# A new written order for the head and the first thirteen tiles of an attention and channel-mix kernel

## The chip, the cores and the metric

The kernel runs on one core of a Trainium2 chip. The metric is the device time in microseconds of one execution. A core has five engines, each with a queue of its own that is worked off in order: PE (matmul), DVE (vector), ACT (scalar, with exponentials), POOL (a second, slower vector engine) and SP (which issues transfers here). Engines wait for each other by semaphores.

## The reference

Attention over keys that are pooled 4 by 4, and a channel mix of its output. There are 4 batches of 12,288 tokens with 128 channels; the keys of a batch, which are also its values, are 768.

```python
kv_pool = kv.reshape(B, H // r, r, W // r, r, C).mean(axis=(2, 4))
k = v = kv_pool.reshape(B, -1, C) @ w_sr
s = scale * (q @ k.transpose(0, 2, 1))
a = np.exp(s - s.max(-1, keepdims=True)); a /= a.sum(-1, keepdims=True) + 1e-09
x = a @ v
x_prev = x shifted by one token
xk = mu_k * x + (1.0 - mu_k) * x_prev
xr = mu_r * x + (1.0 - mu_r) * x_prev
k = np.maximum(xk @ w_k, 0.0)                 # 128 -> 1024
out = 1.0 / (1.0 + np.exp(-(xr @ w_r))) * (k * k @ w_v)
```

## The kernel before, in words

The tokens are worked on in 97 tiles: the first 512 tokens as two tiles of 256 (0 and 1), then 95 tiles of 512. All products are made with operands split in a high and a low part, so most matmuls come in threes (high by low, low by high, high by high).

A tile goes through these steps; the names stand in the tables of the order and, in part, in the trace. *Scores:* load `qf` (SP), split it into `qh` (ACT) and `ql` (POOL); for each 128 tokens s the scores `S0` to `S3` on PE, their maximum `nm` (DVE), the exponential `ex` (ACT, the trace's `pe`), the reciprocal of the sum `rc` (two small DVE instructions), and the normalised weights in two parts, `f1` (ACT) and `f2` (DVE), both `pp` in the trace; `tt` transposes them by DMA into `pT`. *Values:* `AV0` to `AV5` on PE (`px`). *Mix:* `xek` and `xer` on ACT scale `px` by the token scales `s`; `xk` and `xr` on DVE add the shifted part; `xkh`, `xrh` (DVE) and `xkl`, `xrl` (POOL) split them. *Channel mix*, for four groups f of 256 hidden channels: `ha`, `hb` on PE (`ph`), `r` on ACT (`rr`), the product `k2` on DVE (`kk`, or `ph` in place, for one group on ACT), its split `kh` and `kl`, and `va`, `vb` on PE (`pv`). *Gate:* `z` on PE (`pz`), `E` and `th` on ACT, `E1`, `T1` and `g` on DVE, the product `o` on DVE, the store `so`.

Tiles 0 to 8 take their scores from `ksh`, `ksl` and `ksb`. From tile 9 on ACT scales `qf` first (`qs`), POOL clips it (`qg`), and the scores come from `vv`, the scaled keys in two parts. All else is the same.

Ahead of the tiles stands the head: the weights are loaded and split (`wvh`, `wkl` and so on), the first batch's keys and values are loaded, pooled and projected (`pa`, `pb` on PE with fillers of `warm`), split (`ksh`, `ksl`, `ksb`), and the scales are found: `am`, the maximum over the keys (`ex<-ks` in the trace), `ex`, `exi`, `es`, `ivs` after it, `vv` from these; `dg`, `xm` (POOL and PE), `xt` and its reciprocal `xi` (DVE), and `sv` with `s` (POOL) for the token scales. `busy0` and `busy1` are 7 and 6 matmuls of 256 columns (`pw`) whose result nobody reads.

Buffers go round in rings: PSUM has three buffers called `big` (scores, `ph`, the pooled keys), one for `px`, `pz` and `xm`, one for `pv`. In SBUF there are 2 of `qf`, `qh` and `ql`, 4 of `pe` and `pp`, 2 of `pT`, 3 of `kk`, 4 of `kh` and `kl`, 2 of `rr`.

What sets the order is a table of numbers. Each step is put into a heap under its number (lines 68 to 79), and all are issued from the smallest number to the largest; `Ordered` (lines 33 to 45) keeps that order on each engine. The number is a place in the order, not a time at which something happens. `ONCE` (line 921) holds the head's numbers, `EARLY` those of the first tiles, one table for each, `WHEN` those of every later tile, to which i times `PERIOD` is added for tile i, and `LATE` those of the last four. A table also decides which buffer a step gets, since rings hand out theirs in the order of issue.

```python
    def add(self, when, name, fn, of):
        heapq.heappush(self.heap, (when, next(self.count), fn, name, of))
    def give(self):
        while self.heap:
            heapq.heappop(self.heap)[2]()
```

Of the kernel before, what the change touches and what calls it, by code (L numbers as in the profile page):

```python
# [1239 lines left out]
```

## Time and profile before

| | us |
|---|---|
| median of 3 executions | 1860.04 |
| the three | 1862.19, 1859.86, 1860.04 |
| the profiled execution | 1862.46 |
| its span (first to last instruction) | 1860.70 |
| outside the span | 1.76 |
| PE busy | 1844.8 (99%) |
| DVE busy | 1765.7 (95%) |
| ACT busy | 1715.5 (92%) |
| POOL busy | 1229.2 (66%) |

The granted TensorE clock is 0.999 of full over the span. All steps have line 43 in the trace, since one helper records them; instructions are told apart by their tile's name. A row of a timeline has the start, the duration, the engine, the operation with its output and inputs, and in brackets how long the engine had been idle ahead of it and who ended that. Neighbouring instructions of one engine overlap a little in these rows: the start of one to the start of the next is some hundredths of a microsecond less than a duration. In rows of the scores and of `ph` the output is named by its buffer's step.

The span has a head of some 28 us to the first scores, a stretch up to some 210 us in which the first eleven or so tiles come into step, the steady stretch of 18.8 us per tile, and a tail of some 20 us.

### The profile page before, as it was taken

What the parts mean: (1) busy time and instruction counts of PE and PEld (TensorE: products, weight loads), DVE (VectorE), ACT (ScalarE), POOL (GpSimd) and SP (SyncE); (2) the same over time, 40 slices, a digit from 0 to 9 for tenths busy, and PEclk for the clock granted to TensorE, in tenths of its full rate; (3) what the DMA queues carried; (4) which work ended last, traced back from release to release, by engine and by line L of the source; (5) the groups of instructions that cost most, each with busy time, mean ns of one, the idle gap of its engine ahead of it and who ended that gap; (6) DMA issues with size and microseconds to landing.
All of it is one profiled execution on the core that took longest, in us unless ns stands there. A gap on an engine that the chain in (4) does not pass through costs nothing.

```text
span 1860.7 us, 27187 instructions
## 1 busy us (share of the span) xinstructions
PE 1844.8 (99%) x9175; PEld 903.8 (49%) x9175; DVE 1765.7 (95%) x2554; ACT 1715.5 (92%) x2448; POOL 1229.2 (66%) x885
## 2 busy tenths in 40 slices
PE   8999999999999999999999999999999999999999
PEld 5544444444444444444444444444444444444444
DVE  7999999999999999999999999999999999999997
ACT  6999899999999999999999999999999999999997
POOL 2565666676667676767667676767676767676665
PEclk9999999999999999999999999999999999999999
DMA  7866566555556666655656566655574556555552
GB/s 247 157 132 148 117 131 131 108 119 117 119 110 143 135 144 137 129 110 112 124 108 142 131 147 133 145 117 113 105 129 102 119 108 114 113 110 117 103 108 57
DMA packets 644380, 232.16 MB, mean 125 GB/s; under 512 B 612368, under 2 KB 613392, under 8 KB 644240
## 3 DMA queue, kind: packets, MB, share of 16 engines
q1 hardware_dynamic: 644240, 230.43, 59.2%
q8 instruction: 72, 1.18, 0.3%
q14 instruction: 68, 0.56, 0.1%
HBM read 52.63 MB, written 25.17 MB: 42 GB/s over the span
## 4 chain that ended last, share of the span: by engine, by line
PE 85%; DVE 2%; ACT 1%; issue 1%; POOL 0%; DMA 0%; SPq 0%; ACTq 0%; DVEq 0%
PE pv L43 24%; PE ph L43 23%; PE px L43 17%; PE S L43 17%; PE pz L43 3%; DVE pp L43 0%; ACT pp L43 0%; ACT rr L43 0%; DVE nm L43 0%; PE pk L43 0%; ACT pe L43 0%; ACT kh L43 0%; DMA qf<-qT 0%; ACT kk L43 0%; DVE xr L43 0%
## 5 line engine op out<-in xcount | busy, mean ns | idle before, releaser
L43 POOL TENSOR_TENSOR kl<-kk,kh 128x1024 bf16<-128x1024 f32 (+1 forms) x291 | 681.6, 2343 | 51.9 <-DVE kh L43 14.6
L43 DVE SCALAR_TENSOR_TENSOR pp<-pe,rc,pp 128x768 f16<-128x768 f32 x384 | 430.4, 1140 | 3.6 <-ACT pp L43 0.9
L43 PE MATMUL px<-pT,vT 128*128 128x512 f16 (+1 forms) x1746 | 422.0, 378 | 1.1 <-DMA pT<-pp 1.1
L43 ACT ACTIVATE rr<-ph 128x1024 f32<-128x1024 f32 (+1 forms) x388 | 389.1, 1004 | 17.4 <-PE ph L43 16.1
L43 DVE TENSOR_REDUCE nm<-S 128x1 f32<-128x768 f32 x384 | 363.1, 947 | 39.2 <-PE S L43 37.6
L43 ACT ACTIVATE pe<-S,nm 128x768 f32<-128x768 f32 x384 | 344.3, 897 | 43.4 <-DVE nm L43 41.6
L43 ACT ACTIVATE pp<-pe,rc 128x768 f16<-128x768 f32 x384 | 338.8, 927 | 40.4 <-ACT pe L43 37.3
L43 PE MATMUL S<-vv,qg 128*128 128x512 f16 (+1 forms) x1408 | 324.7, 326 | 0.0
L43 ACT ACTIVATE kh<-rr 128x1024 f16<-128x1024 f32 (+1 forms) x291 | 303.6, 1044 | 8.9 <-ACT rr L43 0.4
L43 PE MATMUL pv<-kh,wvl 128*128 128x512 f16 (+1 forms) x784 | 292.6, 375 | 2.4 <-DVE o L43 2.4
L43 PE MATMUL ph<-xkh,wkl 128*128 128x512 f16 (+1 forms) x776 | 292.4, 377 | 1.1 <-ACT pe L43 0.9
L43 PE MATMUL pv<-kh,wvh 128*128 128x512 f16 (+1 forms) x784 | 292.6, 375 | 0.0
L43 PE MATMUL ph<-xkh,wkh 128*128 128x512 f16 (+1 forms) x776 | 292.3, 377 | 0.0
L43 PEld LDWEIGHTS <-vT 128*128 128x128 f16 x1746 | 171.1, 98 | 201.7 <-issue 1.7
L43 POOL TENSOR_SCALAR qg<-qf 128x512 f16<-128x512 f32 x88 | 82.3, 935 | 266.5 <-ACT qf L43 266.5
L43 DVE TENSOR_TENSOR kk<-ph,rr 128x1024 f32<-128x1024 f32 (+1 forms) x194 | 233.8, 1205 | 5.6 <-ACT rr L43 5.3
L43 POOL TENSOR_TENSOR xrl<-xr,xrh 128x512 f16<-128x512 f32 (+1 forms) x97 | 112.0, 1154 | 192.1 <-DVE xrh L43 189.2
L43 PEld LDWEIGHTS <-wvh 128*128 128x128 f16 x1568 | 153.2, 98 | 169.3 <-issue 2.6
L43 PEld LDWEIGHTS <-wkh 128*128 128x128 f16 x1552 | 152.0, 98 | 171.5 <-issue 1.6
L43 PE MATMUL S<-vv,ql 128*128 128x512 f16 x704 | 229.4, 326 | 1.8 <-DVE kk L43 0.8
L43 PE MATMUL ph<-xkl,wkh 128*128 128x512 f16 (+1 forms) x776 | 228.9, 377 | 0.0
L43 PE MATMUL pv<-kl,wvh 128*128 128x512 bf16 (+1 forms) x784 | 228.1, 375 | 0.0
(129 smaller groups left out, 2444.4 us busy)
## 6 DMA issues: line engine op xcount, KB each, us to landing
qf<-qT SPq DMA_DIRECT2D x95, 256.0 KB, 3.5
outT<-o SPq DMA_DIRECT2D x94, 256.0 KB, 3.0
kvt<-kvw SPq DMA_DIRECT2D x36, 512.0 KB, 4.1
pT<-pp SPq DMA_TRANSPOSE x384, 3.8
kva<-kv SPq DMA_DIRECT2D x8, 512.0 KB, 8.9
kvb<-kv SPq DMA_DIRECT2D x4, 512.0 KB, 7.3
raw<-moe_w_v SPq DMA_DIRECT2D x2, 512.0 KB, 4.5
raw<-moe_w_k SPq DMA_DIRECT2D x2, 512.0 KB, 8.2
```

Of the source, the lines that this page charges most:

```text
L43: return self.tc.keep_in_program_order(op(*args, **kwargs))
```

## The change

The head's table `ONCE` has a new number for every step. `EARLY` has thirteen tables in the place of nine: new ones for tiles 0 to 8, and four for tiles 9 to 12, which had the numbers of `WHEN`, with 19.3 added for each tile, before. `KV`, `F1` and `F2`, which say by tile on which engine some steps run, get four entries more of the same content. No step is added, taken away or put on another engine; every step of these tiles stands in a new place of the order. Two lines of the difference:

```diff
-F1 = (('AAAA', 'AAAA', 'AAAA', 'AAAA', 'AAAA', 'AAAA', 'AAAA', 'AAAA', 'AAAA'), 'AAAA', 'AAAA')
+F1 = (('AAAA', 'AAAA', 'AAAA', 'AAAA', 'AAAA', 'AAAA', 'AAAA', 'AAAA', 'AAAA', 'AAAA', 'AAAA', 'AAAA', 'AAAA'), 'AAAA', 'AAAA')
...
-    "sv": 44.377, "tv": 49.805, "wh_wv0": 68.259, "wd_wv0": 69.344, "busy0": 76.581,
+    "xt": 115.0748, "sv": 132.7708, "busy1": 147.7444, "uz": 158.4997, "wd_wr0": 159.6197,
```

**The first batch's keys on DVE.** `kvb` are sums of the pooled keys, `wkl` a weight's low part, `ksl` the keys' low part (512 and 256 columns), `ex<-ks` the maximum `am`, and `nm` the first maxima of scores. Before:

```order
L43 SCALAR_TENSOR_TENSOR wkl<-top,gain_wk,wkh 128x512
L43 TENSOR_TENSOR kvb<-kvb 128x512 x3
L43 SCALAR_TENSOR_TENSOR ksl<-pk,ksh 128x512
L43 TENSOR_REDUCE ex<-ks 128x1
L43 SCALAR_TENSOR_TENSOR ksl<-pk,ksh 128x256
L43 TENSOR_SCALAR ex<-ex 128x1
L43 TENSOR_SCALAR exi<-ex 128x1
L43 TENSOR_SCALAR es<-exi 128x1
L43 RECIPROCAL ivs<-es 128x1
L43 TENSOR_REDUCE nm<-S 128x1 x2
L43 SCALAR_TENSOR_TENSOR vv<-ks,ivs,vv 128x768
L43 TENSOR_REDUCE xt<-xm 128x2
```

Now:

```order
L43 TENSOR_TENSOR kvb<-kvb 128x512
L43 SCALAR_TENSOR_TENSOR wkl<-top,gain_wk,wkh 128x512
L43 SCALAR_TENSOR_TENSOR ksl<-pk,ksh 128x512
L43 SCALAR_TENSOR_TENSOR ksl<-pk,ksh 128x256
L43 TENSOR_REDUCE ex<-ks 128x1
L43 TENSOR_SCALAR ex<-ex 128x1
L43 TENSOR_SCALAR exi<-ex 128x1
L43 TENSOR_SCALAR es<-exi 128x1
L43 RECIPROCAL ivs<-es 128x1
L43 TENSOR_REDUCE nm<-S 128x1 x3
L43 TENSOR_SCALAR rc<-sm 128x2
L43 RECIPROCAL rc<-rc 128x2
```

The second `ksl` has come ahead of `am`. One `kvb` sum fewer stands behind the first `wkl`, and `xt` no longer follows the second `nm`: it stands further down.

**The same engine further on.** `pp` are the low parts of normalised weights, `xt` and `xi` what the token scales come from. Behind the fourth `nm` and the first `vv`, now:

```order
L43 SCALAR_TENSOR_TENSOR pp<-pe,rc,pp 128x768
L43 TENSOR_REDUCE nm<-S 128x1
L43 TENSOR_SCALAR rc<-sm 128x2
L43 RECIPROCAL rc<-rc 128x2
L43 SCALAR_TENSOR_TENSOR pp<-pe,rc,pp 128x768
L43 TENSOR_REDUCE nm<-S 128x1 x2
L43 SCALAR_TENSOR_TENSOR pp<-pe,rc,pp 128x768
L43 TENSOR_REDUCE xt<-xm 128x2
L43 TENSOR_SCALAR rc<-sm 128x2
L43 RECIPROCAL rc<-rc 128x2
L43 SCALAR_TENSOR_TENSOR pp<-pe,rc,pp 128x768
L43 RECIPROCAL xi<-xt 128x2
```

Before, `xt` was the second row behind the first two `nm`, and `xi` came behind one more of them. Now seven `nm`, three `pp` and the `vv` are ahead of `xt`, and one more `pp` ahead of `xi`.

**The token scales on POOL.** `sv` and `s_93` are the token scales, `ql` and `wvl` low parts of queries and a weight, `dg` what `xm` is made from. Before:

```order
L43 TENSOR_TENSOR wvl<-top,wvh 128x512
L43 TENSOR_TENSOR ql<-qf,qh 128x256
L43 TENSOR_SCALAR dg<-ident,ex,mtop 128x128 x2
L43 TENSOR_TENSOR ql<-qf,qh 128x512
L43 MEMSET xek 128x1
L43 TENSOR_SCALAR sv<-xi,es 128x2
L43 TENSOR_SCALAR s_93<-mix,sv 128x2 x2
L43 TENSOR_TENSOR ql<-qf,qh 128x512
L43 TENSOR_TENSOR wvl<-top,wvh 128x512
L43 TENSOR_TENSOR xkl<-xk,xkh 128x256
```

Now:

```order
L43 TENSOR_TENSOR wvl<-top,wvh 128x512
L43 TENSOR_SCALAR k_390<-amp_wk 128x1
L43 TENSOR_TENSOR cv<-k_390,amp_wv 128x1
L43 TENSOR_TENSOR ql<-qf,qh 128x512
L43 TENSOR_SCALAR dg<-ident,ex,mtop 128x128 x2
L43 TENSOR_TENSOR ql<-qf,qh 128x512
L43 MEMSET xek 128x1
L43 TENSOR_SCALAR sv<-xi,es 128x2
L43 TENSOR_SCALAR s_93<-mix,sv 128x2 x2
L43 TENSOR_TENSOR xkl<-xk,xkh 128x256
```

`sv` and `s_93` have kept their place behind `dg` and the memset of `xek`, but now stand behind the `ql` of both next tiles, and the second `wvl` has come to the front, as has `cv`.

**The scaling of the first `px` on ACT.** `pe` are exponentials, `pp` normalised weights, `qh` high parts of queries, `xek` and `xer` the scaled `px`, `rr` the first group of the channel mix. Before:

```order
L43 ACTIVATE wvh<-top 128x512
L43 ACTIVATE pp<-pe,rc 128x768
L43 ACTIVATE pe,sm<-S,nm 128x768
L43 ACTIVATE pp<-pe,rc 128x768
L43 ACTIVATE pe,sm<-S,nm 128x768
L43 ACTIVATE xer<-px,s_93 128x256
L43 ACTIVATE xek<-px,s_93 128x256
L43 CAST qh<-qf 128x512
L43 ACTIVATE pe,sm<-S,nm 128x768
L43 ACTIVATE pp<-pe,rc 128x768
L43 ACTIVATE pe,sm<-S,nm 128x768
L43 ACTIVATE rr<-ph 128x512
```

Now:

```order
L43 ACTIVATE pp<-pe,rc 128x768 x2
L43 ACTIVATE pe,sm<-S,nm 128x768 x2
L43 ACTIVATE pp<-pe,rc 128x768 x2
L43 ACTIVATE pe,sm<-S,nm 128x768
L43 ACTIVATE xek<-px,s_93 128x256
L43 ACTIVATE xer<-px,s_93 128x256
L43 ACTIVATE pe,sm<-S,nm 128x768
L43 ACTIVATE pp<-pe,rc 128x768
L43 CAST qh<-qf 128x512
L43 ACTIVATE pp<-pe,rc 128x768
L43 ACTIVATE pe,sm<-S,nm 128x768
L43 ACTIVATE rr<-ph 128x512
```

`wvh` is gone from here; it stands ahead of the keys now. `xek` precedes `xer`. Between this pair and the first `rr` stand two exponentials in both orders, and one `pp` before, two now.

**Tiles 8 and 11 on DVE.** The names carry numbers here, since rows read alike otherwise. Before; `nm_2322`, `nm_2363`, `nm_2415` and `nm_2443` are the four maxima of tile 11, `kk_2384` and `kk_2389` products of tile 8, `xk_2340` of tile 9, `o_2451` of tile 7:

```order
L43 TENSOR_TENSOR kk_2384<-ph_2352,rr_2359 128x1024
L43 TENSOR_TENSOR kk_2389<-ph_2371,rr_2387 128x1024
L43 TENSOR_SCALAR E_2182<-E_2182,sc_95 128x512
L43 TENSOR_REDUCE nm_2415<-S_2395 128x1
L43 TENSOR_SCALAR th_2184<-th_2184 128x512
L43 SCALAR_TENSOR_TENSOR E_2182<-th_2184,E_2182 128x512
L43 CAST kh_2438<-kk_2367 128x1024
L43 TENSOR_SCALAR rc_2440<-sm_2337 128x2
L43 RECIPROCAL rc_2440<-rc_2440 128x2
L43 TENSOR_REDUCE nm_2443<-S_2419 128x1
L43 TENSOR_TENSOR o_2451<-pv_2300,E_2182 128x512
```

Now; `nm_2308`, `nm_2360` and `nm_2403` are maxima of tile 11, `kk_2358` and `kk_2412` products of tile 8, `xk_2362` of tile 9:

```order
L43 TENSOR_SCALAR rc_2350<-sm_2276 128x2
L43 RECIPROCAL rc_2350<-rc_2350 128x2
L43 TENSOR_TENSOR kk_2358<-ph_2299,rr_2332 128x1024
L43 TENSOR_REDUCE nm_2360<-S_2342 128x1
L43 SCALAR_TENSOR_TENSOR xk_2362<-px_2251,s4_93,xek_2185 128x512
L43 SCALAR_TENSOR_TENSOR pp_2353<-pe_2277,rc_2350,pp_2353 128x768
L43 SCALAR_TENSOR_TENSOR xr_2397<-px_2251,s4_93,xer_2314 128x512
L43 TENSOR_REDUCE nm_2403<-S_2376 128x1
L43 TENSOR_TENSOR kk_2412<-ph_2365,rr_2399 128x1024
L43 TENSOR_SCALAR rc_2438<-sm_2394 128x2
L43 RECIPROCAL rc_2438<-rc_2438 128x2
L43 SCALAR_TENSOR_TENSOR E_2230<-th_2191,E_2230 128x512
```

Before, both products stood together ahead of the third maximum, and the `E`, `th` and `E` of tile 7 behind. Now one product stands ahead of the third maximum and the other behind the fourth, and `xk` and `xr` of tile 9, which were ahead of both products, are between them. The fourth scores of tile 11 on PE take a bank of `big` that the product `kk_2384` frees in the order before, and `kk_2358` in the new one.

## Rows read from the trace of the kernel before

**Rows 1.** The page, part 1: busy time, share of the span, instructions.

```profile
PE 1844.8 (99%) x9175; PEld 903.8 (49%) x9175; DVE 1765.7 (95%) x2554; ACT 1715.5 (92%) x2448; POOL 1229.2 (66%) x885
```

**Rows 2.** Busy by stretch; behind POOL: PEclk, DMA share, GB/s.

```profile
28.40:57.00 28.60, 24.00 (x149) 15.87 (x149) 25.67 (x47) 26.43 (x53) 12.48 (x21) 0.94 0.86 163
57.00:139.00 82.00, 81.91 (x441) 43.60 (x439) 81.14 (x122) 77.09 (x120) 51.71 (x43) 1.00 0.66 138
139.00:208.00 69.00, 64.93 (x316) 30.59 (x313) 63.49 (x90) 60.53 (x87) 36.10 (x29) 1.00 0.62 138
208.00:330.00 122.00, 121.60 (x599) 58.64 (x600) 120.99 (x168) 113.31 (x159) 84.14 (x59) 1.00 0.59 127
330.00:1840.00 1510.00, 1509.29 (x7450) 729.34 (x7449) 1443.06 (x2064) 1413.97 (x2002) 1029.70 (x720) 1.00 0.59 120
```

**Rows 3.** The longest wait of PE: start, duration, operation, [idle before <- releaser].

```profile
191.48 0.38 PE L43 MATMUL pv<-kh,wvl 128*128 128x512 f16 x1 [2.00 <-DVE o L43]
```

**Rows 4.** Timeline of DVE, the pooled keys to the first maximum.

```profile
28.73 0.69 DVE L43 SCALAR_TENSOR_TENSOR ksl<-pk,ksh 128x512 bf16<-128x512 f32 x1 [1.10 <-ACT ks L43]
29.53 0.95 DVE L43 TENSOR_REDUCE ex<-ks 128x1 f32<-128x768 f32 x1
30.40 0.41 DVE L43 SCALAR_TENSOR_TENSOR ksl<-pk,ksh 128x256 bf16<-128x256 f32 x1
...
31.36 1.80 DVE L43 TENSOR_REDUCE nm<-S 128x1 f32<-128x768 f32 x2
```

**Rows 5.** Timeline of ACT, first tiles.

```profile
42.23 0.62 ACT L43 ACTIVATE wvh<-top 128x512 f16<-128x512 f32 x1
...
46.15 0.48 ACT L43 ACTIVATE xer<-px,s 128x256 f32<-128x256 f32 x1
46.51 0.49 ACT L43 ACTIVATE xek<-px,s 128x256 f32<-128x256 f32 x1
```

**Rows 6.** Timeline of PE, start-up of the first tile.

```profile
48.44 0.27 PE L43 MATMUL ph<-xkh,wkl 128*128 128x256 f16 x1 [0.94 <-ACT pe L43]
...
50.35 1.33 PE L43 MATMUL px<-pT,vT 128*128 128x256 f16 x6 [1.09 <-DMA pT<-pp]
51.48 0.42 PE L43 MATMUL ph<-xkh,wkl 128*128 128x256 f16 x1
```

**Rows 7.** Timeline of DVE, start-up of the first tile.

```profile
44.14 2.87 DVE L43 SCALAR_TENSOR_TENSOR pp<-pe,rc,pp 128x768 f16<-128x768 f32 x3
...
54.88 0.69 DVE L43 TENSOR_TENSOR kk<-ph,rr 128x512 f32<-128x512 f32 x1 [1.02 <-ACT rr L43]
56.60 0.69 DVE L43 TENSOR_TENSOR kk<-ph,rr 128x512 f32<-128x512 f32 x1 [1.03 <-ACT rr L43]
```

**Rows 8.** Timeline of POOL, the token scales.

```profile
36.23 0.26 POOL L43 TENSOR_SCALAR sv<-xi,es 128x2 f32<-128x2 f32 x1
36.59 2.13 POOL L43 TENSOR_SCALAR s<-mix,sv 128x2 f32<-128x2 f32 x2
```

**Rows 9.** Timeline of PE: eighteen px of 512 columns, and what follows.

```profile
72.35 4.05 PE L43 MATMUL px<-pT,vT 128*128 128x512 f16 x18
76.24 0.38 PE L43 MATMUL ph<-xkh,wkl 128*128 128x512 f16 x1
```

**Rows 10.** DVE by form, 30 to 330 us: count | busy us, mean ns.

```profile
L43 DVE TENSOR_TENSOR kk<-ph,rr 128x1024 f32<-128x1024 f32 x27 | 32.9, 1217 | 2.5 <-ACT rr L43 2.3
...
L43 DVE SCALAR_TENSOR_TENSOR xr<-px,s,xer 128x512 f32<-128x512 f32 x14 | 10.3, 739 | 0.0
...
L43 DVE TENSOR_SCALAR rc<-sm 128x2 f32<-128x2 f32 x34 | 7.9, 233 | 1.6 <-ACT pe L43 1.6
L43 DVE TENSOR_SCALAR E<-E,sc 128x512 f32<-128x512 f32 x13 | 6.8, 523 | 0.0
L43 DVE CAST xkh<-xk 128x512 f16<-128x512 f32 x14 | 6.7, 475 | 0.0
L43 DVE TENSOR_SCALAR th<-th 128x512 int32<-128x512 int32 x13 | 6.3, 485 | 0.0
```

**Rows 11.** Timeline of DVE and POOL near 186: a short operation beside kl.

```profile
185.99 2.14 POOL L43 TENSOR_TENSOR kl<-kk,kh 128x1024 bf16<-128x1024 f32 x1
...
186.24 1.91 DVE L43 TENSOR_SCALAR rc<-sm 128x2 f32<-128x2 f32 x1 [0.70 <-ACT pe L43]
```

More of the change, by code (lines that the diff above doesn't have):

```diff
@@ L885 @@
 CAST = {'k': 'D', 'r': 'D'}
-KV = (('1123', '1123', '1123', '1123', '1123', '1123', '1123', '1123', '1123'), '1123', '1123')
+KV = (('1123', '1123', '1123', '1123', '1123', '1123', '1123', '1123', '1123', '1123', '1123', '1123', '1123'), '1123', '1123')
 KC = 64
@@ L891 @@
 FIRST = {'wd': {'wk': 'DD', 'wv': 'GG', 'wr': 'G'}, 'vl': 'D', 'dg': 'P', 'add': {'a': 'PPPPDDDD', 'b': 'DDDD'}, 'kh': 'A', 'kb': 'A', 'homes': [[0, 0], [0, 2], [0, 4], [1, 0], [1, 2], [1, 4], [2, 0], [3, 0]]}
-F1 = (('AAAA', 'AAAA', 'AAAA', 'AAAA', 'AAAA', 'AAAA', 'AAAA', 'AAAA', 'AAAA'), 'AAAA', 'AAAA')
-F2 = (('DDDD', 'DDDD', 'DDDD', 'DDDD', 'DDDD', 'DDDD', 'DDDD', 'DDDD', 'DDDD'), 'DDDD', 'DDDD')
+F1 = (('AAAA', 'AAAA', 'AAAA', 'AAAA', 'AAAA', 'AAAA', 'AAAA', 'AAAA', 'AAAA', 'AAAA', 'AAAA', 'AAAA', 'AAAA'), 'AAAA', 'AAAA')
+F2 = (('DDDD', 'DDDD', 'DDDD', 'DDDD', 'DDDD', 'DDDD', 'DDDD', 'DDDD', 'DDDD', 'DDDD', 'DDDD', 'DDDD', 'DDDD'), 'DDDD', 'DDDD')
 WARM = 62
@@ L921 @@
 ONCE = {
[10 rows of a table removed]
-    "wx_wk": -44.637, "wy_wk": -43.552, "wx_wr": -42.466, "ws_wk1": -41.381, "wy_wr": -40.295,
[11 rows of a table removed]
[12 rows of a table added]
+    "wy_wk": -21.0485, "pa2": -19.6873, "mix": -18.3260, "wg_wv": -16.9648, "L_b0": -15.6036,
[10 rows of a table added]
 }
@@ L947 @@
     {
[13 rows of a table removed]
-    },
-    {
[5 rows of a table removed]
-        "xck": 155.102, "xk": 156.187, "xkh": 158.811, "xrh": 163.119, "xkl": 164.196,
[8 rows of a table removed]
-    },
-    {
[16 rows of a table removed]
-    },
-    {
[16 rows of a table removed]
-    },
-    {
[7 rows of a table removed]
-        "xek": 185.966, "xer": 186.726, "xr": 186.853, "xk": 188.5, "xkh": 201.206, "xkl": 202.273,
[8 rows of a table removed]
-    },
-    {
[7 rows of a table removed]
-        "xer": 206.116, "xek": 206.422, "xk": 206.881, "xr": 207.492, "xkh": 207.645,
-        "xrh": 207.798, "xkl": 207.849, "xrl": 216.451, "ha0": 223.292, "hb0": 223.412,
[7 rows of a table removed]
-    },
-    {
[7 rows of a table removed]
-        "xek": 224.726, "xr": 225.203, "xk": 225.323, "xkh": 226.398, "xrh": 227.471,
[8 rows of a table removed]
-    },
@@ L1068 @@
-    {
[7 rows of a table removed]
-        "xer": 234.731, "xcr": 234.763, "xr": 234.795, "xek": 234.994, "xk": 234.995,
-        "xkh": 240.079, "xkl": 240.741, "ha1": 248.17, "hb1": 248.692, "xrh": 249.215,
[7 rows of a table removed]
-    },
-    {
[7 rows of a table removed]
-        "xek": 253.447, "xr": 254.294, "xck": 254.297, "xk": 254.3, "xkh": 259.322, "xrh": 260.589,
[8 rows of a table removed]
[5 rows of a table added]
+        "xek": 145.0219, "xer": 149.1056, "xk": 153.1893, "xkh": 154.5505, "xkl": 155.9118,
[9 rows of a table added]
+    },
+    {
[5 rows of a table added]
+        "xr": 158.9263, "xek": 159.2997, "xck": 159.5663, "xk": 159.9397, "xkh": 160.0997,
[9 rows of a table added]
+    },
@@ new lines @@
+    {
[7 rows of a table added]
+        "AV0": 162.8730, "xek": 163.2463, "xk": 163.2997, "xkh": 163.4063, "xkl": 163.4597,
[9 rows of a table added]
+    },
+    {
[7 rows of a table added]
+        "AV2": 173.0046, "xcr": 175.6809, "xer": 177.2687, "xek": 179.0078, "xk": 180.3991,
+        "xr": 180.5730, "xkh": 181.0947, "xrh": 184.3991, "xkl": 186.0311, "xrl": 191.8633,
[8 rows of a table added]
+    },
+    {
[7 rows of a table added]
+        "AV3": 193.3214, "xer": 195.1440, "xek": 196.1562, "xck": 196.5102, "xr": 197.0765,
+        "xk": 197.1473, "xrh": 198.6341, "xkh": 198.7049, "ha2": 199.2712, "xkl": 199.3420,
[8 rows of a table added]
+    },
@@ new lines @@
+    {
[8 rows of a table added]
+        "xr": 203.5190, "xkh": 203.7314, "xrh": 204.4784, "xrl": 206.4962, "xkl": 211.1373,
[8 rows of a table added]
+    },
+    {
[8 rows of a table added]
+        "xkh": 219.0130, "xkl": 219.6530, "xr": 221.2530, "xrh": 222.8530, "ha2": 235.1130,
[8 rows of a table added]
+    },
+    {
[7 rows of a table added]
+        "xer": 239.0597, "xck": 239.3797, "xek": 239.5930, "xcr": 240.8730, "xk": 241.8330,
+        "xr": 242.3663, "xrh": 246.1747, "xrl": 248.3178, "xkh": 249.4868, "xkl": 250.0713,
[8 rows of a table added]
+    },
+    {
[7 rows of a table added]
+        "AV3": 252.2144, "xek": 252.9937, "xer": 256.7730, "xcr": 259.7730, "xr": 260.7730,
+        "xk": 261.2730, "xkh": 263.5571, "ha0": 264.5767, "xkl": 265.0354, "xrh": 265.1374,
[8 rows of a table added]
+    },
@@ L1103 @@
+    {
[7 rows of a table added]
+        "AV4": 264.6276, "xcr": 264.8825, "AV0": 265.0864, "xek": 265.4942, "xer": 265.9020,
[10 rows of a table added]
+    },
+    {
[7 rows of a table added]
+        "AV0": 283.1671, "AV4": 283.4812, "xcr": 292.9055, "xer": 294.7698, "xek": 295.0366,
+        "xk": 296.3707, "xkh": 296.6375, "xkl": 296.9044, "xr": 297.1712, "xrh": 304.4853,
[9 rows of a table added]
+    },
+    {
[8 rows of a table added]
+        "xer": 312.1917, "xr": 314.7727, "xrh": 317.4034, "xkh": 318.9100, "xkl": 322.5215,
[9 rows of a table added]
+    },
+    {
[18 rows of a table added]
     },
```

376 rows, old and new, of tables (EARLY, ONCE) are left out of this document.

## The prediction

> **What bounds the kernel now.** I read the page's busy times first, then the busy table cut into stretches, then PE's and DVE's timelines where that table shows gaps, and last the mean of each kind of DVE instruction. The busy line gives PE 1844.8 us, 99% of the span, and DVE 1765.7 us, 95% [rows 1]: PE sets the time, DVE is close behind. The stretches show where PE is not full [rows 2]. From 330 to 1840 us PE works 1509.29 of 1510 us, and that stretch runs in the steady order, which the change leaves alone. From 57 to 139 us it works 81.91 of 82, with DVE at 81.14 beside it. From 208 to 330 it lacks 0.40. So PE's idle time lies in two places: 28.60 - 24.00 = 4.60 us from 28.4 to 57 us, and 69.00 - 64.93 = 4.07 us from 139 to 208 us. After 208 us PE runs through, so the end moves by what the new order does to PE's waits before that point, plus the moment at which its first scores start. All PE waits together are 4.60 + 0.09 + 4.07 + 0.40 = 9.2 us; no order of the same work can gain much more.
>
> In the second place PE waits for DVE: the longest wait is 2.00 us, `pv` for the product `o` [rows 3]. DVE itself idles 69.00 - 63.49 = 5.51 us in this stretch and 0.86 in the one ahead of it [rows 2], 6.37 us in all. So PE waits for a DVE that was late because it had waited, on ACT: a DVE-bound kernel in its first 200 us, PE-bound after.
>
> **The start: pooled keys to first maximum.** On DVE the 768-column maximum `ex` over the pooled keys (0.95 us, at 29.53) stands between the two differences `ksl`, and the first maximum of scores starts at 31.36 [rows 4]. In the new order both `ksl` come first. The wait of PE for the second one goes, `ex` moves behind it, and the first `nm` has the four tiny operations ahead of it as before. ACT no longer has the weights' `wvh` (0.52 from its start to the next one's, as at 42.23 [rows 5]) between the keys of the second half. What still holds is the last load and the pooled additions, of which the same number stands in front. From 28.73 the DVE chain is 0.69 + 0.41 + 0.95 + some 0.6 for the tiny ones, that is 31.4 if no step waits less, and 0.8 earlier if the chain starts that much sooner, because `ksl` waited 1.10 us for ACT [rows 4]. I take the larger part: -0.7, between -1.5 (all of the 1.10, and the overlap of neighbours) and +0.7 (the two `qh` casts now stand ahead of `ks` on ACT, and wait for a load).
>
> **Start-up of the first tile.** At 48.44 PE starts the first `ph`, after 0.94 us of waiting; at 50.35 it waits 1.09 for a transposed `pT`; and at 51.48 a 256-column matmul takes 0.42 instead of 0.27 us [rows 6]. DVE then idles 1.02 and 1.03 us, for `rr` from ACT [rows 7]: 2.05 us which the DVE-bound part behind never gets back. What the first `ph` needs is `xek` on ACT, at 46.51 [rows 5], then DVE's `xk` and `xkh`: 48.44 - 46.51 = 1.93 us. In the new order ACT has eight exponentials and six `pp` ahead of `xek`, as many as before; `wvh` (0.52) and `xer` (0.36, from 46.15 to 46.51) have left, and the start is 0.7 earlier: ACT is ready at 46.51 - 0.52 - 0.36 - 0.7 = 44.9. The new price is on POOL and DVE: `xek` needs the token scales `s`, which POOL made in 0.36 + 2.13 = 2.5 us at 36.23, long ahead [rows 8]. Now `xt` and `xi`, from which they come, stand behind seven maxima, three `pp`, one `vv`, and the `rc` between them, and one more `pp` comes between `xt` and `xi`. Two maxima take 1.80 us [rows 4] and three `pp` 2.87 [rows 7]: seven times 0.87, four times 0.95, one `vv` as another 0.95, and 1.1 for `rc` and `xt` make 11.9 us. From a first maximum at 30.7 that is 42.6, and s is ready at 42.6 + 2.5 = 45.1, if DVE never waits. So `xek` starts near 45.2 and `ph` near 47.2, 1.2 us earlier, with 0.2 us to spare at most. Two more things speak for the new order: `xk` and `xkh` now stand together, and PE has a `px` group to do beside the first `ph`. I take -1.5 of the 2.05, between -2.05 and +2 (scales late; priced below).
>
> Beside this stands a second effect, that of the filler matmuls: seven of the thirteen now come ahead of the first scores, where PE waits for keys anyway. Their place among the scores held 7 x 0.11 us. The granted clock is 0.94 in this stretch and 1.00 behind it [rows 2]; the 0.42 us matmul ran at the lower of the clock's two levels, and it came after the two waits of 0.94 and 1.09 us. The Trainium skill (TensorE: Matmul & The Clock Gate, Part 1, What's actually happening) says that the throttled clock is the default and activity lifts it; by that rule removing fillers from a stretch with waits risks the lower level, and keeping PE fed there is worth more than its work. The trace agrees in that the lower level follows the waits; it doesn't show the order without fillers.
>
> **From 57 to 208 us.** DVE idled 6.37 us here, in single waits for ACT's `rr` and exponentials. The new order re-sorts every step of thirteen tiles, so each of these waits can go, stay, or come back under another name. A bound from below is that all go (-6.4), from above that none does (0). The stretch from 208 to 330, in the old steady order, has a DVE idle of 1.01 in 122 us [rows 2], at which rate 151 us would have 1.2: good orders exist. I take half, -3.2, the middle between ends for which no row decides.
>
> **What the order itself asks.** One thing can be counted, since each engine keeps its program order: how much PE has to do before it needs a product of DVE, and how much DVE must do before it gives it. PE's fourth scores of tile 11 need a bank of `big` that a product of tile 8 frees. In the new order there stand ahead of them on PE one `ha`, two `va` (four matmuls each), two `hb`, one `vb` (two each) and one `z` (three) fewer: 3 x 4 + 3 x 2 + 3 = 21 matmuls of 512 columns. Eighteen `px` of that width run from 72.35 to 76.24, 0.216 each [rows 9]: 4.5 us less work. On DVE the product has one `kk`, one `xk`, one `xr` and one `xkh` fewer ahead of it, and one `E`, one `th` and one `rc` pair more: 1.22 + 0.74 + 0.74 + 0.48 less 0.52 + 0.49 + 0.40 (its reciprocal taken as another 0.17) [rows 10] is 1.77, or 1.7 with the overlap of neighbours. So PE is there 4.5 - 1.7 = 2.8 us earlier than DVE is, against the same place of before. There it wasn't that place that bound but the `o` of tile 7, by 0.2 us more when both queues are added up alike. The excess is +2.6; counted with the fillers of the old order left in it is +1.7, and with DVE's longer steps beside a busy POOL +3.4. I take +2.4. It is a price that PE pays by waiting, and it hides only where DVE's idle time above is cut by more.
>
> **Sum.** -0.7 - 1.5 - 3.2 + 2.4 = -3.0. The profiled execution took 1862.46 us, its span 1860.70, 1.76 outside it; the median of the three runs, 1860.04, lies 2.42 below that execution. With -3.0 the span is 1857.7, such an execution 1859.5, and the median 1857.0. POOL has the same work; SP issues the same loads and transposes, with DMA busy 0.86 of the time up to 57 us and 0.59 to 0.66 behind it [rows 2], so a load that moves by a few places has room after 57 us, hardly before.
>
> A POOL instruction in a new place can cost by itself. At 186.24 an `rc` of two columns took 1.91 us on DVE, against a mean of 0.23, and it ended with the `kl` that POOL had run from 185.99 for 2.14 us [rows 10, 11]. The Trainium skill (SBUF - State Buffer, SBUF: two separate sides) tells of a port pair of VectorE and GpSimd that one holds for its whole instruction; this row agrees. By that rule every new neighbourhood of the two is a draw, of 1.7 us per such collision by the row; the old order has one of them right ahead of PE's 2.00 us wait, and the new one may lose it or gain another. It stands in no term, and widens the range.
>
> **The rivals.**
> *The waits go altogether.* The mutual waits of DVE, ACT and PE vanish: -0.7 - 2.05 - 6.4 + 2.4 = -6.7, a median of 1853.3. For it speaks the stretch from 57 to 139 us, where the old order already ran 82 us with both engines full; against it that thirteen tiles have to fit one another, at 99% of two engines.
> *Given back.* DVE stays as late as before, since the waits for ACT come back elsewhere: ACT is busy 60.53 of 69 us from 139 to 208 [rows 2], and each `rr` moved ahead puts an exponential back. Then -0.7 - 1.0 + 0 + 2.4 = +0.7: 1860.7, no change.
> *Scales from POOL late (slower).* `xi` waits behind seven maxima and four `pp`. If DVE waits 3 us among them (for an exponential that a `pp` needs), s comes at 48.1 and `ph` at 50.1, 1.7 later than before. It decides from the point where `xek` starts later than 46.5. DVE's 2.05 us of idling grow to some 3.8, PE idles ahead of `ph` with no filler there, and the lower clock's level costs again about 0.15 us for each of some ten matmuls: -0.7 + 1.7 + 1.5 + 0 + 2.4 = +4.9 with no gain behind, a median of 1864.9; with a small gain behind 1864.
> *It doesn't do what it says* is excluded: the same steps stand on each engine, in another order.
>
> **How the numbers follow.** The forecast has 0.40, around 1857.0 with its own range of 1855 to 1859; all waits gone 0.25; given back 0.19; scales late 0.16. 0.2%, 3.7 us, is about what a measurement of this kernel tells from no change: faster is below 1856.3, slower above 1863.8. Faster: 0.25 and 0.15 of the forecast's 0.40, which straddles 1856.3, 0.40. Slower: 0.16 and 0.04 of the case given back, 0.20. The same: 0.25 + 0.15, 0.40. The range, 1852.5 to 1864.5, takes in all waits gone and nearly the late scales, and leaves out some 0.1 at each end.
>
> **What would show it.** Right: the first `nm` at 30.2 to 31; the first `ph` at 47 to 47.6, with no `kk` waiting 1 us for `rr` behind it; DVE's idle from 57 to 208 us near 3; a wait of PE's scores for `kk` around tile 11. Wrong: `xek` waiting for POOL's s (the start-up term and with it the forecast); a DVE as idle as before (given back); PE without a wait up to 208 us (the order's price then was none). The prediction falls if PE's waits up to 330 us, 9.2 us before, don't come down to about 6 to 7.

## The result, and the profile after

The new order takes 1878.95 us (median of four, 1877.63 to 1879.89) against 1859.95: 1.0099 of the time before, 95% interval 1.0082 to 1.0117. It is slower by 19 us; the forecast was 1857.0, with a range up to 1864.5. The profiled execution took 1879.0, its span is 1877.2, 16.5 more than before.

The page's busy line of the new order, which answers to [rows 1]:

```profile
PE 1841.4 (98%) x9067; PEld 902.6 (48%) x9175; DVE 1783.2 (95%) x2554; ACT 1715.3 (91%) x2448; POOL 1224.1 (65%) x885
```

The count of DVE's instructions is the same, 2554, and they take 17.5 us more. That is about the 16.5 us by which the span grew, and it is the row that tells where to look: the same operations take longer each. (108 matmul records are missing from this trace, so its PE sum isn't compared.)

Busy time by stretch, as in [rows 2]:

```profile
28.40:57.00 28.60, 22.39 (x145) 14.64 (x147) 26.03 (x45) 24.09 (x47) 16.31 (x25) 1.00 0.77 148
57.00:139.00 82.00, 74.13 (x390) 39.11 (x395) 81.03 (x115) 71.42 (x111) 42.17 (x39) 1.00 0.61 129
139.00:208.00 69.00, 67.33 (x327) 32.24 (x331) 66.87 (x93) 61.94 (x90) 38.86 (x30) 1.00 0.57 123
208.00:330.00 122.00, 114.00 (x539) 53.54 (x545) 118.58 (x151) 102.89 (x144) 73.16 (x54) 0.99 0.58 129
330.00:1840.00 1510.00, 1504.17 (x7374) 729.81 (x7456) 1447.16 (x2071) 1416.69 (x2009) 1026.81 (x718) 1.00 0.59 121
```

PE now lacks 6.2, 7.9, 1.7 and 8.0 us in the first four stretches, 23.8 in all, against 9.2. (Some 17 of the missing matmul records, counted by the weight loads beside them, make about 1 us of this, an estimate: the last stretch lacks 5.8 us with 82 missing.) DVE fills its time from 57 to 139 us, 81.03 of 82, as before, but with 115 instructions in place of 122. It isn't waiting; it is slow.

Which instructions are slow shows in the table by form, 30 to 330 us (count, busy us, mean ns). First the new order:

```profile
L43 DVE SCALAR_TENSOR_TENSOR pp<-pe,rc,pp 128x768 f16<-128x768 f32 x62 | 72.4, 1183 | 0.4 <-ACT pp L43 0.4
L43 DVE TENSOR_REDUCE nm<-S 128x1 f32<-128x768 f32 x64 | 59.9, 947 | 2.2 <-PE S L43 2.0
L43 DVE TENSOR_TENSOR kk<-ph,rr 128x1024 f32<-128x1024 f32 x26 | 31.4, 1216 | 0.7 <-ACT rr L43 0.5 <-issue 0.3
...
L43 DVE TENSOR_REDUCE acc<-kvt 128x64 f32<-128x1024 f32 x12 | 14.5, 1207 | 0.0
L43 DVE CAST kh<-kk 128x1024 f16<-128x1024 f32 x12 | 11.8, 980 | 0.0
L43 DVE TENSOR_SCALAR rc<-sm 128x2 f32<-128x2 f32 x32 | 10.8, 338 | 0.2 <-ACT pe L43 0.2
...
L43 DVE SCALAR_TENSOR_TENSOR E<-th,E 128x512 f32<-128x512 f32 x12 | 9.5, 793 | 0.1
...
L43 DVE TENSOR_SCALAR th<-th 128x512 int32<-128x512 int32 x12 | 7.9, 656 | 0.0
...
L43 DVE RECIPROCAL rc<-rc 128x2 f32<-128x2 f32 x32 | 5.3, 166 | 1.1
```

and the forms of the old order that [rows 10] doesn't have:

```profile
L43 DVE SCALAR_TENSOR_TENSOR pp<-pe,rc,pp 128x768 f16<-128x768 f32 x66 | 73.4, 1130 | 0.2 <-ACT pp L43 0.2
L43 DVE TENSOR_REDUCE nm<-S 128x1 f32<-128x768 f32 x68 | 63.8, 945 | 0.3 <-PE S L43 0.2
...
L43 DVE TENSOR_REDUCE acc<-kvt 128x64 f32<-128x1024 f32 x12 | 14.5, 1210 | 0.0
...
L43 DVE CAST kh<-kk 128x1024 f16<-128x1024 f32 x13 | 8.9, 681 | 0.0
L43 DVE SCALAR_TENSOR_TENSOR E<-th,E 128x512 f32<-128x512 f32 x13 | 8.8, 681 | 0.1
...
L43 DVE RECIPROCAL rc<-rc 128x2 f32<-128x2 f32 x34 | 5.6, 166 | 1.2
```

Maxima, products with PSUM, sums and reciprocals have the same mean to 3 ns or so. `kh` went from 681 to 980 ns, `th` from 485 to 656, `rc` from 233 to 338, `E<-th` from 681 to 793, `pp` from 1130 to 1183. The timeline of the last place where PE waits long shows what happens to them (all engines; start, duration, operation):

```profile
274.87 2.13 POOL L43 TENSOR_TENSOR kl<-kk,kh 128x1024 bf16<-128x1024 f32 x1
274.94 2.62 DVE L43 CAST kh<-kk 128x1024 f16<-128x1024 f32 x1
...
277.47 0.94 DVE L43 TENSOR_REDUCE nm<-S 128x1 f32<-128x768 f32 x1
...
278.34 1.20 DVE L43 TENSOR_REDUCE acc<-kvt 128x64 f32<-128x1024 f32 x1
...
279.30 2.13 POOL L43 TENSOR_TENSOR kl<-kk,kh 128x1024 bf16<-128x1024 f32 x1
279.46 2.25 DVE L43 TENSOR_SCALAR th<-th 128x512 int32<-128x512 int32 x1
...
285.17 0.39 PE L43 MATMUL ph<-xkh,wkl 128*128 128x512 f16 x1 [3.58 <-DVE kl L43]
```

`kh` starts 0.07 us behind a `kl` of POOL, which runs to 277.00, and ends at 277.56: POOL's rest and then its own 0.6. The maximum and the sum behind it run undisturbed. `th`, 0.42 us when alone, meets the next `kl` and takes 2.25. At 285.17 PE has waited 3.58 us for DVE, and from there to the end its waits are 1.6 us in all. The granted clock is 0.66 from 285 to 290 us, behind this wait, and 1.00 ahead of it and after. It is the row of [rows 11] again, many times over.

The same collision has another side. In the order before, in its steady stretch:

```profile
238.96 2.38 DVE L43 SCALAR_TENSOR_TENSOR pp<-pe,rc,pp 128x768 f16<-128x768 f32 x2
...
240.42 2.92 POOL L43 TENSOR_TENSOR kl<-kk,kh 128x1024 bf16<-128x1024 f32 x1
```

Here the second `pp` is under way when `kl` starts, and it is POOL that takes longer, 2.92 us for 2.13. Up to 330 us ten `kl` of the old order took 2.75 to 2.93 us in this way, and four of the new. POOL is busy 66% of the span, DVE 95%: the old order lets the engine pay that has time left. No run tests what that alone is worth.

To compare kernels I add up, from the first to the 73rd maximum of scores, by how much each DVE instruction is longer than its form usually is (the duration that a tenth of that form's instructions in the two traces stay below). I call this the excess. It is 15.70 us before and 32.02 after. The same stretch then closes like an account: the first maximum comes 1.89 us later (33.25 for 31.36), DVE's idle time is 1.88 less (9.94 for 11.82), the excess 16.32 more, together 16.3; the 73rd maximum comes 16.7 later, at 371.62 for 354.94. Of the excess, instructions beside a POOL `kl` make 5.1 us before (7 of them), 20.5 after (18); an instruction counts as beside the POOL instruction that it overlaps longest, if it is over 0.15 us longer than usual. With every one over 0.1 us longer that overlaps a `kl` at all it is 8.9 and 22.9, so the growth is 14 to 15 us either way.

### The profile page after: what moved, and what is told of

Read it like the earlier page. It is cut to its first block, busy times and chain, and to the rows that moved or that the text cites. A ratio compares the mean times of both kernels' runs of the same rounds, so it can differ in the third digit from the quotient of the medians.

```text
span 1877.2 us, 27084 instructions
## 1 busy us (share of the span) xinstructions
PE 1841.4 (98%) x9067; PEld 902.6 (48%) x9175; DVE 1783.2 (95%) x2554; ACT 1715.3 (91%) x2448; POOL 1224.1 (65%) x885
## 4 chain that ended last, share of the span: by engine, by line
PE 78%; DVE 3%; ACT 2%; issue 2%; POOL 0%; ACTq 0%; DVEq 0%
PE ph L43 22%; PE pv L43 21%; PE S L43 16%; PE px L43 16%; PE pz L43 4%; DVE pp L43 1%; ACT pp L43 1%; ACT rr L43 1%; DVE nm L43 0%; DVE kl L43 0%; ACT pe L43 0%; ACT kh L43 0%; DVE xk L43 0%; DVE xr L43 0%; PE pk L43 0%
## 5 line engine op out<-in xcount | busy, mean ns | idle before, releaser
L43 ACT ACTIVATE rr<-ph 128x1024 f32<-128x1024 f32 (+1 forms) x388 | 388.7, 1003 | 15.7 <-PE ph L43 14.7
L43 PE MATMUL ph<-xkh,wkl 128*128 128x512 f16 (+1 forms) x776 | 292.1, 377 | 10.6 <-DVE kl L43 5.4
L43 PE MATMUL pv<-kl,wvh 128*128 128x512 bf16 (+1 forms) x685 | 205.9, 374 | 0.7
```

The source lines that it names most:

```text
L43: return self.tc.keep_in_program_order(op(*args, **kwargs))
```

## The experiments

Two theories stood at the start. *Stalls*: the new order sets DVE's short operations beside long POOL instructions, and they wait for POOL's end. *Order*: PE and DVE wait for each other by the order of the steps, and DVE's longer instructions only fill time that would be waited anyway. A third, *head*, blames the later first maximum. The table has what came of the runs; excess and idle are DVE's, by the account above, busy is the page's. The old order was timed again beside each set of runs, with medians from 1859.95 to 1861.36, and a ratio is to the one of its own set.

| kernel | median us | ratio to the old order, 95% | DVE busy | excess | DVE idle | first maximum |
|---|---|---|---|---|---|---|
| old order | 1860.4 | | 1765.7 | 15.7 | 11.8 | 31.36 |
| new order | 1878.95 | 1.0099 [1.0082, 1.0117] | 1783.2 | 32.0 | 9.9 | 33.25 |
| new, no kl | 1861.64 | 1.0004 [0.9995, 1.0013] | 1764.2 | 13.6 | 12.4 | 31.39 |
| old, no kl | 1859.24 | 0.9994 [0.9985, 1.0002] | 1761.1 | 11.3 | 13.5 | 30.78 |
| new, no kl in tiles 0 to 5 | 1869.8 | 1.0049 [1.0036, 1.0061] | 1772.6 | 22.6 | 12.4 | 31.55 |
| new, no kl in tiles 6 to 12 | 1869.33 | 1.0046 [1.0032, 1.0059] | 1773.9 | 22.7 | 10.0 | 32.96 |
| new, kl in halves | 1871.14 | 1.0056 [1.0043, 1.0069] | 1777.6 | 27.1 | 8.8 | 31.66 |
| new, kl in quarters | 1872.61 | 1.0063 [1.0051, 1.0076] | 1778.0 | 28.2 | 9.9 | 31.91 |
| old, kl in halves | 1862.8 | 1.0011 [1.0003, 1.0020] | 1766.9 | 19.7 | 10.3 | 31.29 |
| new, eleven steps moved | 1870.59 | 1.0054 [1.0042, 1.0067] | 1774.5 | 25.0 | 10.5 | 31.57 |
| new, seven more moved | 1870.12 | 1.0052 [1.0038, 1.0066] | 1768.4 | 17.8 | 15.6 | 32.07 |
| new tiles, old head | 1882.06 | 1.0117 [1.0101, 1.0132] | 1783.8 | 33.7 | 10.3 | 35.34 |
| old, one more POOL instruction a tile | 1879.44 | 1.0100 [1.0086, 1.0114] | 1784.1 | 37.1 | 10.3 | 30.90 |
| new, kl as memsets | 1871.95 | 1.0059 [1.0046, 1.0072] | 1776.7 | 27.0 | 8.3 | 31.32 |

**POOL's kl left out, in both orders.** In the new order:

```diff
@@ plan_tile, kl
+                if kv[f] != "3" and i < 13:
+                    st[f"kl{f}"] = nil if W == T else nil[:, :2 * W].rearrange("p (h t) -> p h t", h=2)
+                    return
                 (dve if kv[f] == "3" else pool).tensor_tensor(
```

> The new order with POOL's subtraction kl left out in the first thirteen tiles (its readers take a tile of zeros). Theory stalls (the new order puts short DVE operations beside long POOL instructions, and they wait for POOL's end): DVE instructions are 32.0 us longer than their undisturbed length from the first to the 73rd maximum of scores, about 18 us of it beside kl; without kl some 10 to 15 us are left, and the time falls from 1879 to 1862 to 1868 us. Theory order (PE and DVE wait for each other by the order of the steps, and the longer DVE instructions only fill time that would be waited anyway): the time stays at 1875 us or more.

In the old order, the same edit:

> The old order with the same subtraction left out in the same tiles. Theory stalls: the old order has 15.7 us of longer DVE instructions over the same stretch, 5 to 8 us of it beside kl; the time falls from 1860 to 1854 to 1858 us, so that the distance of new to old order falls from 19 us to 6 to 12. Theory order: the old order's time hardly moves (1858 to 1860) and the distance stays above 15 us.

The new order falls by 17.3 us to 1861.64, the old one by 1.2 (its interval holds no change), and of the distance of 19 us 2.4 is left, less than the 6 to 12 that the theory of stalls had asked for; the old order's own time is where the theory of order had put it. The page of the new order without `kl`:

```profile
PE 1842.2 (99%) x9175; PEld 902.7 (49%) x9175; DVE 1764.2 (95%) x2554; ACT 1715.6 (92%) x2448; POOL 1143.8 (62%) x847
```

DVE's 2554 instructions are back at 1764.2 us. The theory of order is out as the main cause. But the new order isn't ahead without the stalls either: it is 2.4 us behind, with the first maximum 0.6 later, 2.3 more of excess and 1.1 less of idle time. One thing this run can't tell apart: leaving `kl` out also shortens POOL's queue for the steps behind it, and PE's `vb` no longer waits for it. Two of the changes below, the added instruction and the moved steps, keep every `kl`.

**One half of the tiles at a time.** The same edit with `i < 6`, and with `6 <= i < 13`:

> The new order with POOL's kl left out in tiles 0 to 5 alone (their readers take zeros). Between the 13th and the 29th maximum the longer DVE instructions are 11.6 us in the new order, 3.1 in the old. If what DVE loses early is carried to the end, the time falls by 8 to 11 us, to 1868 to 1871; if PE and DVE are held early by other waits of the order (the moved steps of the second kind won back nothing there), it falls by 0 to 4 us, to 1875 to 1879.

> The new order with POOL's kl left out in tiles 6 to 12 alone. Between the 45th and the 61st maximum the longer DVE instructions are 13.8 us in the new order, 3.4 in the old. If the late ones set the end (the last wait of PE comes at 285 us), the time falls by 9 to 14 us, to 1865 to 1870; if both halves count alike, each gives 8 to 9 of the 17 us that all of them gave, 1870 to 1871; if the early ones are needed too, it falls by less than 5 us.

Each gives 9.2 to 9.6 us, and 18.8 together is about what all of them gave (17.3). The pages' DVE sums fall by 10.6 and 9.3. So what DVE loses to POOL at 80 us is carried to the end as fully as what it loses at 280: PE is late by then and, with only 1.6 us of waits after 285 us, never makes it up.

**More of the cost, in the old order.** The order of PE, DVE and ACT stays; POOL gets one instruction more in each of eleven tiles, whose result nobody reads:

```diff
@@ plan_tile, kl
+                if f == 0 and W == T and i < 13:
+                    pool.tensor_tensor(out=junk, in0=st[f"kk{f}"], in1=st[f"kh{f}"], op=ALU.subtract)
```

> The old order, with one more subtraction on POOL for each of the first tiles of 512 tokens, behind that of the first group, its result read by nobody: 2.13 us of POOL more in each of eleven tiles, nothing else changed. Theory stalls: DVE's short operations meet it at places that nobody chose; the longer DVE instructions rise from 15.7 to 20 to 26 us, the time from 1860 to 1862 to 1868 us. Theory order: PE, DVE and ACT have the same work in the same order, POOL is busy two thirds of the time: 1859 to 1861.5 us.

It costs 18 to 19 us, more than was expected; POOL is then 67% busy, from 66. DVE's idle time doesn't grow (10.3 us for 11.8), so it isn't that POOL gives `kk` and `kh` back later. DVE's page sum is 18.4 us up:

```profile
PE 1849.8 (98%) x9175; PEld 903.9 (48%) x9175; DVE 1784.1 (95%) x2554; ACT 1715.8 (91%) x2448; POOL 1253.3 (67%) x896
```

17.7 us of the excess lie beside these eleven instructions, 1.6 us for each that stands where nobody chose; beside `kl`, which they shift, it is 9.1 in the place of 5.1. Two of them, with what DVE did there:

```profile
139.66 2.14 POOL L43 TENSOR_TENSOR junk<-kk,kh 128x1024 bf16<-128x1024 f32 x1
...
139.78 3.76 DVE L43 SCALAR_TENSOR_TENSOR pp<-pe,rc,pp 128x768 f16<-128x768 f32 x2
...
145.49 2.14 POOL L43 TENSOR_TENSOR junk<-kk,kh 128x1024 bf16<-128x1024 f32 x1
...
145.65 2.00 DVE L43 TENSOR_SCALAR rc<-sm 128x2 f32<-128x2 f32 x1
```

Two `pp` take 3.76 us, 1.8 more than at the rate of [rows 7], where three take 2.87, and an `rc` of two columns 2.00. By this the old order is remarkable for what it didn't have: 39 `kl` with 1024 columns stand in its first 330 us, and beside all `kl` it lost 5.1 us, some 0.13 each.

**The instruction cut.** With halves (`for c in range(2)` over 512 columns), then quarters, in the new order, and halves in the old:

> The new order, each kl of the first thirteen tiles on POOL cut into two instructions of 512 columns (1.16 us each in the trace, against 2.13 for the whole). Theory stalls: a DVE operation waits at most for the end of one half; the 32.0 us of longer DVE instructions fall to 18 to 24, the time from 1879 to 1866 to 1872 us. Theory order: the same work in the same order, POOL a little longer: 1878 to 1881 us.

> The new order, each kl of the first thirteen tiles cut into four instructions of 256 columns (0.67 us each for such a form in the trace, 2.7 in all against 2.13). Theory stalls: DVE waits for a quarter at most, so less than with halves (1871.1 us, 27.1 us of longer instructions): 1863 to 1870 us, 18 to 25 us, unless POOL itself gets late by its longer work. Theory order: no gain over the halves, rather a loss by POOL's longer work, 1871 to 1876.

> The old order with the same cut. Theory stalls: 15.7 us of longer DVE instructions fall to 9 to 13, the time from 1860 to 1855 to 1859 us. Theory order: 1859 to 1861 us.

Halves win 7.8 us in the new order, as expected, though the excess falls to 27.1 only. Quarters don't win more: 31 stalls beside `kl` in the place of 18, each shorter, 14.3 us together against 20.5 whole and 14.8 in halves. In the old order halves lose: the cut moves every end of a POOL instruction, and the excess rises to 19.7 us, 6.8 of it beside `kl`. These two are misses of the expectation that a shorter instruction always costs less; the quarters' time is even where the theory of order had put it. In these runs the place counts more than the length.

**DVE's steps moved, all else in the new order.** Eleven numbers in `EARLY` (and that of one transpose, which follows its step):

```diff
@@ EARLY, examples
-"T1": 165.2197   +"T1": 167.3601      (tile 1: behind nm, acc, kk)
-"kh2": 200.6872  +"kh2": 200.8299     (tile 3: behind kk and ph)
-"rc3": 300.1062  +"rc3": 303.4099     (tile 12: behind acc and kk)
```

> The new order with eleven of DVE's short steps moved back by one to three places in DVE's queue, behind an operation that reads PSUM (nm, kk, acc, o, kl): T1 of tile 1, f21 of tile 5, kh2 of 3, f23 of 6, f21 of 7, xrh and E1 of 6, f21 and kh2 and T1 of 11, rc3 of 12. These eleven were 15.4 us longer beside POOL than undisturbed. All other engines keep their order. Theory stalls: half or more of it goes, some comes back at other places: 1864 to 1873 us, and the longer DVE instructions fall from 32 to 18 to 26 us. Theory order: eleven places in DVE's queue are too little to change what PE waits for: 1876 to 1881 us.

8.4 us are won by eleven swaps in one queue, with every instruction kept. Seven more in the same manner:

> The new order with the eleven steps moved, and seven of DVE's steps moved back again in the order that the first moves left (rc3 of tiles 4 and 5, T1 of 3, xrh of 6, f20 of 8, kh2 of 12, and f21 of 5 behind rc3; one step of ACT, f13 of tile 5, keeps its place behind rc3): these were 9.8 us longer than undisturbed in that run. Theory stalls: a third to a half of it stays gone, so 1864 to 1869 us after 1870.6, and 17 to 23 us of longer DVE instructions after 25.0. Theory order: 1869 to 1873.

This fell short. The excess went down by another 7.2 us, to about what the old order has, and the time by nothing: DVE's idle time rose by 5.1, and its first maximum came 0.5 later. DVE's waits in that run, 31 to 330 us (us in total, times, longest):

```profile
DVE kk L43 <- ACT rr L43: 3.6, 6, 1.5
DVE nm L43 <- PE S L43: 1.9, 3, 0.9
DVE pp L43 <- ACT pp L43: 1.5, 2, 1.1
DVE ph L43 <- ACT rr L43: 1.4, 2, 0.9
```

It waits for ACT's `rr` and for PE; that the stalls had covered these waits before is a reading, not a test. So the theory of order has a part: with its stalls at the old level the new order is still some 9 us behind. How much of that is the order itself, and how much the places to which I moved the steps, no run here tells apart.

**The old head with the new tiles.** Table `ONCE` of before, all else of after:

> The old order of the head (table ONCE) with the new order of the thirteen tiles. Theory stalls: they lie in the tiles' order, so this stays slow, 1872 to 1880 us, with 25 to 33 us of longer DVE instructions. Theory head (the first maximum came at 33.25 us instead of 31.36, the tiles fall out of step behind it and meet POOL by that): with the old head 1860 to 1866 us.

1882.06 us, 2 above what the theory of stalls had asked for; the theory of the head is out. The old head doesn't suit these tiles: their first maximum is at 35.34.

**POOL busy without reading.** Each `kl` of the tiles of 512 is replaced by `pool.memset(kl, 0.0)`, twice:

> The new order with each kl of the first tiles of 512 on POOL replaced by two memsets of the same tile (the low part is zero then; an estimate of 0.9 us each from the 128x128 memset's 0.20), so POOL is busy as long at the same places but reads nothing. If any POOL instruction holds DVE up, the time stays near 1879 us and the longer DVE instructions near 30 us; if only POOL instructions that read two operands do, it is as without kl, 1860 to 1864 us and 12 to 16 us.

Neither expectation holds: 1871.95 us, with an excess of 27.0. The rows tell why. Two pairs of memsets stand on POOL here, 0.97 us each:

```profile
177.02 3.87 POOL L43 MEMSET kl<- 128x1024 bf16 x4
...
177.17 0.82 DVE L43 TENSOR_SCALAR rc<-sm 128x2 f32<-128x2 f32 x1
...
178.03 0.17 DVE L43 RECIPROCAL rc<-rc 128x2 f32<-128x2 f32 x1
...
178.11 1.93 DVE L43 SCALAR_TENSOR_TENSOR pp<-pe,rc,pp 128x768 f16<-128x768 f32 x2
...
179.95 1.47 DVE L43 CAST kh<-kk 128x1024 f16<-128x1024 f32 x1
...
181.35 0.94 DVE L43 TENSOR_REDUCE nm<-S 128x1 f32<-128x768 f32 x1
```

`rc` and `kh` are held up, to the end of a memset; the reciprocal and both `pp` aren't. From 30 to 330 us eight `pp` started beside a memset and none was longer; of the eight that started beside a `kl` that reads, in the new order, seven were, by 7.5 us in all, and the eighth met only its last 0.08 us. So there are two kinds of DVE operation that POOL stops in these runs: casts and `rc`, `th`, `E<-E`, which have one operand tile (`E<-E` with scalars beside it) and which a memset stops as a subtraction does, and `pp`, whose two tiles lie in SBUF, which a memset doesn't stop. `E<-th` was stopped by a `kl` (1.60 us at 252.37); none started beside a memset, so which kind it is isn't shown.

## Why the prediction was wrong

- **The step that failed** is the paragraph on POOL beside DVE. It read the right row, 1.91 us for an `rc` beside `kl`, priced one collision at 1.7 us, called every new neighbourhood a draw, and then put it in no term: 0, with a wider range. The draw isn't even. The trace of the old order already said so: of its 39 long `kl` in the first 330 us few held DVE up, 7 by the count above. An order in which nothing places them loses more, and the term was +16.3 us of DVE's time, 15.4 of it beside `kl`. It is also the only effect large enough to leave the range, which was widened for one or two collisions, not for eighteen. The prediction's own sign of falling came true by it: PE's idle time up to 330 us went from 9.2 to some 23, not to 6 to 7.
- **The gains, -3.0 in all, didn't come either.** Without `kl`, the nearest to an order without that term, the new order is 2.4 us behind the old one. Which of the other terms that is stays open; the table has 0.6 at the start and 2.3 of other excess.
- **The rule of the Trainium skill** (SBUF - State Buffer, SBUF: two separate sides) was the one that spoke against the change, and was cited for a range instead of a rival. The same page of the Trainium skill says more than the prediction took from it, under Who interferes with whom: of copy, cast and `tensor_scalar` that they can enter the mode that contends, of a DVE instruction with two SBUF inputs that it contends only with a GpSimd instruction that reads SBUF, and of `tensor_reduce` that it never does on trn2. The traces agree on each: `kh`, `th` and `rc` (0.30, 0.17 and 0.10 us more in the mean), `pp` beside `kl` and beside a memset, `nm` and `acc` (947 for 945 ns, 1207 for 1210).
- **The start, -0.7.** Wrong in sign: 33.25 for 31.36. The second `ksl` waited 0.94 us for ACT's `ksh`, and `am` 0.45 for `ks`. It isn't the two `qh` casts that held ACT: they end at 28.30, and ACT then idles 1.54 us until DVE's first `ksl` is done, for which its `ks` waits; `ksh` stands behind `ks`, and the second `ksl` needs `ksh`. In this execution a `wkl` met POOL's `wvl` as well and took 1.65 us.

```profile
27.56 1.65 DVE L43 SCALAR_TENSOR_TENSOR wkl<-top,gain_wk,wkh 128x512 f16<-128x512 f32 x1
...
29.84 0.60 ACT L43 ACTIVATE ks<-pk 128x512 f32<-128x512 f32 x1 [1.54 <-DVE ksl L43]
...
30.75 0.42 DVE L43 SCALAR_TENSOR_TENSOR ksl<-pk,ksh 128x256 bf16<-128x256 f32 x1 [0.94 <-ACT ksh L43]
31.62 0.95 DVE L43 TENSOR_REDUCE ex<-ks 128x1 f32<-128x768 f32 x1 [0.45 <-ACT ks L43]
...
33.25 0.94 DVE L43 TENSOR_REDUCE nm<-S 128x1 f32<-128x768 f32 x1
```

In the runs that keep this head and the first tiles' order, the first maximum came at 31.3 to 32.1 in seven of eight; in the eighth, at 32.96, `wkl` took 1.69 us too. The four runs of the old head and tiles have it at 30.8 to 31.4. So the new start is some 0.6 us later in the mean, and the rest is that stall. The bound of +0.7 has this size by luck, since it was set for the casts.
- **The start-up, -1.5.** The mechanism held, and the size nearly: DVE's idle time from the first maximum to 57 us is 1.04 us, 2.39 before, so -1.35. From the first maximum the first `ph` comes 16.33 us later, 17.08 before: -0.75.

```profile
45.73 0.16 DVE L43 RECIPROCAL xi<-xt 128x2 f32<-128x2 f32 x1
...
46.36 0.59 POOL L43 TENSOR_SCALAR s<-mix,sv 128x2 f32<-128x2 f32 x2
...
47.81 0.47 ACT L43 ACTIVATE xek<-px,s 128x256 f32<-128x256 f32 x1
...
49.58 0.28 PE L43 MATMUL ph<-xkh,wkl 128*128 128x256 f16 x1 [0.33 <-ACT pe L43]
```

`xi` came 12.5 us behind the first maximum (11.9 forecast). The scales were ready at 46.95, ahead of ACT, so the rival of late scales didn't happen: POOL needed 0.59 us for the two `s` in place of the 2.13 of [rows 8]. That 2.13 was itself a collision, with POOL as the one that paid: before, the first `s` started at 36.59 beside two `pp` of DVE, took 1.84 us and ended 0.1 us behind them.

```profile
36.40 1.94 DVE L43 SCALAR_TENSOR_TENSOR pp<-pe,rc,pp 128x768 f16<-128x768 f32 x2
```

Of the two waits of about 1 us in [rows 7] one of 0.53 is left. What was feared of the fillers didn't come: the granted clock is 1.00 from 28.4 to 57 us, 0.94 before, and the first `ph` takes 0.28 us.
- **DVE's idle time from 57 to 208 us, -3.2.** It is 0.97 + 2.13 = 3.10 for 6.37, a cut of 3.27. The size is right, though half was chosen with no row for it, which is luck. It bought nothing that shows in the time, since DVE's own instructions grew by more.
- **The order's excess, +2.4.** Not seen at its place: PE's waits of scores for `kk` are 0.5 us in all, two of them. Without `kl` one of 0.59 us comes at 197.01. DVE's idle time from 208 to 330 us did rise, from 1.01 to 3.42, but for scores from PE and other small waits. The count of the steps was right; it took them at undisturbed durations, and DVE's queue didn't run at them.
- **The rivals.** "Given back" had the sign of a DVE that stays late, at 1860.7, by waits; the slow rival had 1864.9, by another cause. The true cause was described as a row and had no chance of its own.

## What to carry to other kernels

When only an order changes, compare the busy time of each engine at equal instruction counts first: 17.5 us more for the same 2554 DVE instructions points at longer instructions before any wait is looked at. Before forecasting such a change, list which operations of one engine are lengthened beside another's in the trace of before, count how many neighbours a careless order would have, and give that its own rival: here some 0.5 to 1.6 us for each long POOL instruction, against 0.13 in the old order. Ask for each collision which engine pays, since in these rows the one that starts second is held. A loss of the second engine was paid in full here, early or late, since the first had next to no idle time left to the end.
